# Loads of the first expert tile's weights tied, chunk by chunk, to successive attention units

## The chip, the cores and the metric

The kernel runs on one core of one Trainium2 chip. The metric is device time in microseconds (us) of that core; a time that is quoted alone is the median of several runs. The profile is one further execution. The matmul engine is called PE, its weight loads PEld, the vector engine DVE, the scalar engine ACT, GpSimd POOL, and the queue from which most DMAs are issued SP.

## The reference: what is computed

Three stages follow one another on 1536 tokens (2 batches of 768, 8 heads of 64). The first is attention in which a query sees only the keys of its own cluster, the second a mixture of 8 experts with one expert per token, the third a two-layer network with a leaky nonlinearity.

```python
mask = q_assign[:, :, :, None] == k_assign[:, :, None, :]
scores = scale * np.matmul(q, k.transpose(0, 1, 3, 2))
attn = softmax(np.where(mask, scores, -1e9)) @ v        # shortened
...
e_idx = np.argmax(x @ w_gate + modality_bias[modality_id], axis=1)
h = np.maximum(x[mask] @ w1[e], 0.0)                    # for every expert e
out[mask] = gate_w[mask, None] * (h @ w2[e])
...
h = x @ w_in
return (np.maximum(h, 0) + alpha * np.minimum(h, 0)) @ w_out
```

## The kernel before

**Attention.** The work is cut into 8 groups (2 batches of 4 head pairs), each of 12 units; a unit is one block of 128 queries against one head's 768 keys. A unit's scores are matmuls on PE (line 944, four of them), then DVE takes the row maximum (951), ACT the exponential (963), the result is split into a high and a low half-precision part (`p`), SP issues one transposing DMA (`pt<-p`, line 980), and PE multiplies the transposed tile with the values (line 988, 12 matmuls). The group before its use is prepared beside this (lines 719 to 911, with copies `s2k<-mt` and `s2q<-mt` by DMA, line 389). After a group its output goes to DRAM (`x_d<-xg`, line 1026). After four groups the batch is routed: logits (1045) and a long chain of small DVE operations that ends in tables of tokens and experts.

**Experts.** Tokens are handled in tiles of 128 with one expert each: 5 tiles of the first batch, 8 main tiles after both. A tile is called a slot. The weights of its expert, 4 MB, go in 8 loads of 512 KB (line 1310) into one buffer `wst` of 8 chunks, chunks 0 to 3 for the first layer (matmuls of line 1379), 4 to 7 for the second (line 1409). The loads of slot 0 always run. Those of every later slot are conditional: they move data only if the expert differs from the slot's before, but they are issued, in order, and wait until the chunk's last reader is done. Slots 0, 1 and 2 multiply straight from `wst`, in single-precision matmuls of two records each, and are meant to lie beside the second batch's attention. From slot 3 on the weights are split into `whl` tiles by ACT and DVE (lines 364 and 392) first. Two weight tiles of the third stage are also prepared in this phase (`wst2`, `tw`, `wf`, lines 1453 to 1470).

**What sets the order.** The program is not written in execution order. Every step is an operation with a priority and a set of predecessors; a planner (`Sched.run`) simulates the engines with costs that are written in the kernel, always picks the operation that can start first, and emits all instructions in the order so found. A predecessor given through `deps` moves the operation in that order; it adds no semaphore. The instruction order on each engine is then fixed, and every engine, SP's queue included, takes its instructions in order. The knobs sit in a table `N`; `units` is a list that collects the score operation of every unit, so `units[57]` is the scores of unit 57. Units 0 to 47 are the first batch.

Of the kernel before, what the change touches and what calls it, by code (L numbers as in the profile page):

```python
# [299 lines left out]
def kernel(  # L300
# [17 lines left out]
    B, H, SEQ, D = q.shape  # L318
# [27 lines left out]
    VW = 2 * D + 2  # L346
    CEXP = 15.0 * math.log(2.0)
    BIG = float(2.0 ** 60)
    N = dict(s1q=2, s1k=2, s2q=2, s2k=2, p=3, p16=5, pt=4, v16=2, wf_early=2, xs=2, whl=3, whl2=3, whi='A', wlo='D', lead=1, tw=1, wdma=1.25, pss=2, ps1=4, sq=1, bd=1.5, bp=0, ulead=4, pa=2, pb=0, nat=3, hi='*', lo='DP', vraw=1, mvp=1, mvb=0, epi=1, rM=2, lob=0.5, mve='PA', wd=0.3, wa=0.03, wp=0.03, wpl=0.03, cs=1, back=2, nld=8, dsame=0.127, lump='cs', mp=90, mps=8, mpn=0, trp=0.5, evp=3, xTs2=0, xtp=9, fl=6, rsh=1, rp0=0, go=-4, so=0, pre=0, fws=5, gs=4, gsl=1, xsl=0)
    W_EARLY = N["wf_early"]  # L350

    S = Sched()
    S.back = N["back"]
    S.DSAME = N["dsame"]
    S.win = {"DVE": N["wd"], "ACT": N["wa"], "PE": N["wp"], "POOL": N["wpl"]}
    S.bias = {"DVE": N["bd"], "POOL": N["bp"]}
    MV = {"SP": 0.65, "POOL": 1.05} if N["mvp"] else {"SP": 0.65}
    mv_bias = {"POOL": N["mvb"]}
# [38 lines left out]
    def open_pool(name, side="left", space=None, deps=()):  # L397
        def fn(_):
            kw = dict(name=name, bufs=1, side=side)
            if space is not None:  # L400
                kw["space"] = space
            else:
                kw["reuse_waits"] = "tile"
            p = tc.alloc_tile_pool(**kw)
            pools[name] = p
            for r, shape, dt, n in specs.get(name, ()):
                if isinstance(r, Ring):
                    r.tiles += [p.tile(shape, dt, name=f"{r.name}{len(r.tiles) + i}") for i in range(r.n if n is None else n)]
                else:
                    r.t = p.tile(shape, dt, name=r.name)  # L410

        o = S.op({"MEM": 0.0}, fn, deps=deps, prio=-1e9)
        for r, _, _, n in specs.get(name, ()):
            if n is not None:
                o.adds += tuple((r, r.n + i) for i in range(n))
                continue
            r.opened = o
            if isinstance(r, Buf):
                r.state = {None: ([o], [])}
        return o  # L420

    def close_pool(name):
        deps = set()
        for r, _, _, _ in specs.get(name, ()):
            deps.update(r.ops)
            deps.add(r.opened)
        return S.op({"MEM": 0.0}, lambda _: pools.pop(name).release(), deps=deps, prio=-1e9)
# [10 lines left out]
    def tens(pool, name, shape, dt):  # L438
        b = Buf()
        b.name = name  # L440
        specs.setdefault(pool, []).append((b, shape, dt, None))
        return b
# [32 lines left out]
    fl = tens("const", "fl", [P, B, SLOTS[1]], I32)  # L475
# [202 lines left out]
    units = []  # L678
# [237 lines left out]
    pslot = 8.0  # L916
# [370 lines left out]
        r0 = (b * SLOTS[0] + j) * P  # L1287
        return ys_d[r0:r0 + P, :]

    def slot(b, j, p0, always=False, split=False):  # L1290

        S.prio = p0
        S.stream = "moe"
# [1 line left out]
        nl = 8 // N["nld"]  # L1295
        for c0 in range(0, 8, nl):
            def load(e, c0=c0):
                if not reg:
                    reg.append(nc.sync.value_load(ei.t[0:1, b, j:j + 1], min_val=0, max_val=E - 1))
                    if not always:  # L1300
                        reg.append(nc.sync.value_load(fl.t[0:1, b, j:j + 1], min_val=0, max_val=1))
                kw = {} if always else dict(cond=reg[1] > 0)
                dst = wst.t[:, c0:c0 + nl, :]
                if c0 < 4:
                    src = w1[bass.ds(reg[0], 1), c0 * P:(c0 + nl) * P, :].rearrange("a (k p) f -> p (a k) f", p=P)
                else:
                    src = w2[bass.ds(reg[0], 1), (c0 - 4) * 2 * P:(c0 - 4 + nl) * 2 * P, :].rearrange(
                        "a (k p) f -> p (a k) f", p=P)
                    dst = dst.rearrange("p c (k f) -> p (c k) f", k=2)
                nc.sync.dma_start(dst, src, **kw)  # L1310

            S.op({"SP": 0.6 if c0 == 0 else 0.06}, load, r=[(ei, b), (fl, b)], w=[(wst, c0 + x) for x in range(nl)],
                 dma=((2.95 if always else N["wdma"]) * nl / 2, "load"), prio=p0 - 5)
        xs = S.new(r_xs)
        S.op({"POOL": 1.05}, lambda e: nc.gpsimd.indirect_dma_start(
            out=xs.t, out_offset=None, in_=x_d[0:(b + 1) * SEQ, :],
# [12 lines left out]
        whl = []  # L1329
# [76 lines left out]
        for f in range(KF):  # L1406
            def mm2(e, f=f):
                for i, (a, w_) in enumerate(parts):
# [5 lines left out]
                 prio=p0 + (pslot + 0.1 if split and f >= N["fl"] else 0.3))  # L1414
# [138 lines left out]
    NU = len(groups) * UG  # L1553
# [27 lines left out]
    for b in range(B):  # L1581
        for j in range(MAIN[b]):
            m = b * MAIN[0] + j
            if m == N["nat"]:
                o = close_pool("prep")
                o2 = open_pool("moe2", side="right", deps=[o])
                o = close_pool("core")
                o.deps.add(o2)
                open_pool("moe3", side="right", deps=[o, o2])
                open_pool("ffn0", deps=[o])  # L1590
                open_pool("ffnw", deps=[o])

                open_pool("ps2", space=PSUM, deps=[close_pool("pss")])
            slot(b, j, N["mp"] + N["mps"] * m if b == 0 and m < N["mpn"] else NU + 4 + pslot * m, always=m == 0, split=m >= N["nat"])
            rel.append(last[0])

    S.op({"POOL": 0.6}, lambda e: nc.gpsimd.memset(zt.t, 0.0), w=[zt], prio=NU + 4 + pslot * N["nat"])
# [1 line left out]
    for i, (b, j) in enumerate(spare):  # L1599
# [4 lines left out]
         deps=[last[0]])  # L1604
# [20 lines left out]
    with tc.If(nb[B] > 0):  # L1625
        for b in range(B):
            for j in range(MAIN[b], SLOTS[b]):
                with tc.If(nb[b] > j):
                    slot(b, j, 0.0, always=True)
                    now()  # L1630
        for t in range(C):
            gather(t, x2[0], posu, t)
        now()
# [59 lines left out]
```

## Time and profile before

| What | Value |
|---|---|
| median of 3 runs | 768.56 us (765.15 to 773.28) |
| profiled execution | 769.91 us, span 768.1 us |
| PE busy | 670.0 us (87%) |
| DVE / ACT / POOL busy | 553.9 / 416.3 / 354.3 us |
| moved by DMA | 105.21 MB, mean 137 GB/s |

The span is what lies between the first and last instruction; the remaining 1.8 us of the profiled execution lie around it. The program has four stretches: attention of the first batch (to about 200 us), attention of the second with slots 0 to 2 in it (to about 349), slots 3 to 12 (to about 488), and the third stage, in which PE is busy throughout, to the end. An engine that is busy for a part of a stretch is not what bounds it unless something waits for it; so the rows further down are of waits and of stretches.

### The profile page before, as it was taken

What the parts mean: (1) busy time and instruction counts of PE and PEld (TensorE: products, weight loads), DVE (VectorE), ACT (ScalarE), POOL (GpSimd) and SP (SyncE); (2) the same over time, 40 slices, a digit from 0 to 9 for tenths busy, and PEclk for the clock granted to TensorE, in tenths of its full rate; (3) what the DMA queues carried; (4) which work ended last, traced back from release to release, by engine and by line L of the source; (5) the groups of instructions that cost most, each with busy time, mean ns of one, the idle gap of its engine ahead of it and who ended that gap; (6) DMA issues with size and microseconds to landing.
All of it is one profiled execution on the core that took longest, in us unless ns stands there. A gap on an engine that the chain in (4) does not pass through costs nothing. (4 is left out here: it accounts for less than half of the span.)

```text
span 768.1 us, 11996 instructions
## 1 busy us (share of the span) xinstructions
PE 670.0 (87%) x4135; PEld 561.5 (73%) x4135; DVE 553.9 (72%) x902; ACT 416.3 (54%) x677; POOL 354.3 (46%) x333
## 2 busy tenths in 40 slices
PE   4667777777578898899979989799999999999997
PEld 3656667667466766656857878699999988999996
DVE  7798897989868997469999989488888733332231
ACT  6678777687567968547868988122223232111112
POOL 4258676858357866401244320255645643222221
PEclk9899988988679999999999999999999999999999
DMA  7479999979799979991463651134334030000002
GB/s 178 121 134 209 207 198 174 214 128 226 176 193 231 213 147 185 208 359 45 166 227 101 216 210 70 58 115 141 129 110 134 32 110 28 1 0 1 1 1 82
DMA packets 189284, 105.21 MB, mean 137 GB/s; under 512 B 156480, under 2 KB 169920, under 8 KB 189216
## 3 DMA queue, kind: packets, MB, share of 16 engines
q1 hardware_dynamic: 186848, 96.88, 53.5%
q0 software_dynamic: 2368, 7.49, 3.7%
q8 instruction: 35, 0.57, 0.3%
q14 instruction: 33, 0.27, 0.1%
HBM read 87.37 MB, written 12.85 MB: 130 GB/s over the span
## 5 line engine op out<-in xcount | busy, mean ns | idle before, releaser
L1523 PE MATMUL ps<-wf,ghl 128*128 128x512 f32 x576 | 138.2, 392 | 3.1 <-POOL ghl L392 3.1
L1523 PEld LDWEIGHTS ps<-wf,ghl 128*128 128x128 f32 x576 | 107.0, 188 | 25.5 <-POOL ghl L392 4.6
L392 POOL TENSOR_TENSOR ghl<-g,ghl 128x384 fp32r<-128x384 f32 x62 | 70.6, 1145 | 108.1 <-ACT ghl L364 108.0
L364 ACT ACTIVATE ghl<-g 128x384 fp32r<-128x384 f32 x64 | 33.7, 526 | 140.9 <-DVE g L1506 140.6
L1503 DVE TENSOR_SCALAR m<-ps,alp 128x384 f32<-128x384 f32 x64 | 39.3, 614 | 96.8 <-PE ps L1495 94.3
L951 DVE TENSOR_REDUCE nm<-pss 128x1 f32<-128x768 f32 x96 | 90.7, 950 | 19.8 <-PE pss L944 10.6
L963 ACT ACTIVATE p<-pss,nm 128x768 f32<-128x768 f32 x96 | 86.2, 902 | 34.2 <-DVE nm L951 20.1
L392 DVE TENSOR_TENSOR whl<-wst,whl 128x1024 fp32r<-128x1024 f32 x80 | 100.7, 1299 | 3.0 <-ACT whl L364 2.7
L988 PEld LDWEIGHTS <-pt 128*128 128x128 f16 x1152 | 62.3, 102 | 54.4 <-DMA pt<-p 43.5
L988 PE MATMUL ps<-v,pt 128*128 128x129 f16 (+1 forms) x1152 | 70.8, 214 | 32.1 <-DMA pt<-p 29.1
L392 POOL TENSOR_TENSOR p<-p,p 128x768 f16<-128x768 f32 x48 | 83.1, 1737 | 23.3 <-ACT p L364 13.0
L364 ACT ACTIVATE whl<-wst 128x1024 fp32r<-128x1024 f32 x80 | 83.6, 1059 | 13.1 <-PE ps L1409 5.5
L944 PE MATMUL pss<-s1k,s1q 128*128 128x384 f32 x192 | 63.8, 416 | 13.3 <-ACT p L963 13.0
L1495 PE MATMUL ps<-x2a,wf 128*128 128x384 f32 x384 | 69.9, 338 | 1.8 <-ACTq L1625 1.8
L1495 PEld LDWEIGHTS ps<-x2a,wf 128*128 128x128 f32 x384 | 67.7, 188 | 3.3 <-ACTq L1625 2.2
L1495 PE MATMUL ps<-x2b,wf 128*128 128x384 f32 x384 | 69.9, 338 | 0.0
L1495 PEld LDWEIGHTS ps<-x2b,wf 128*128 128x128 f32 x384 | 67.6, 188 | 1.1
L1379 PE MATMUL ps<-whl,xTs 128*128 128x512 f32 x240 | 63.9, 400 | 4.0 <-DVE whl L392 3.8
L1409 PE MATMUL ps<-whl,hTs 128*128 128x512 f32 x240 | 63.0, 399 | 2.4 <-DVE hTs L392 2.3
L373 POOL TENSOR_SCALAR p<-p 128x768 f16<-128x768 f32 x44 | 41.1, 938 | 39.7 <-ACT p L963 27.8
L976 DVE SCALAR_TENSOR_TENSOR p<-p,p 128x768 f16<-128x768 f32 x48 | 58.7, 1234 | 0.1
L944 PE MATMUL pss<-s2k,s2q 128*128 128x384 f32 x192 | 53.7, 363 | 4.3 <-DMA s2q<-mt 4.3
(238 smaller groups left out, 1140.1 us busy)
## 6 DMA issues: line engine op xcount, KB each, us to landing
wst<-in_moe_w_dram SPq DMA_DIRECT2D x104, 512.0 KB
wst<-in_moe_w_in_dram SPq DMA_DIRECT2D x8, 1024.0 KB
wst<-in_moe_w_out_dram SPq DMA_DIRECT2D x8, 1024.0 KB
ys_d<-ys SPq DMA_DIRECT2D x13, 256.0 KB
raw<-in_k_dram SPq DMA_DIRECT2D x8, 384.0 KB
raw<-in_q_dram SPq DMA_DIRECT2D x8, 384.0 KB
vraw<-in_v_dram SPq DMA_DIRECT2D x8, 384.0 KB
x_d<-xg SPq DMA_DIRECT2D x8, 384.0 KB
```

The lines of the kernel that those rows point to most:

```text
L364: nc.scalar.activation(out=out, in_=in_, func=AF.Copy)
L373: nc.gpsimd.tensor_scalar(out=out, in0=in_, scalar1=1.0 if scale is None else scale, scalar2=0.0, op0=ALU.mult, op1=ALU.add)
L392: ENG[e].tensor_tensor(out=out, in0=a, in1=b, op=ALU.subtract)
L944: nc.tensor.matmul(s.t[:, jj, 0:HS], hd["12"[i], "q"].t[:, h, j, qs], hd["12"[i], "k"].t[:, h, jj], start=(i == 0), stop=(i == 1))
L951: S.op({"DVE": c_dve(SEQ)}, lambda e: nc.vector.tensor_reduce(out=nm.t, in_=s.t[:, :, 0:HS], axis=AX.XY, op=ALU.max, negate=True), r=[s], ...
L963: S.op({"ACT": c_act(SEQ) + 0.04}, lambda e: nc.scalar.activation(out=p.t, in_=s.t[:, :, 0:HS], func=AF.Exp, bias=nm.t), r=[s, nm], w=[p])
L976: S.op({"DVE": c_dve(SEQ)}, lambda e: nc.vector.scalar_tensor_tensor(out=p16.t[:, 1, :], in0=pf(), scalar=PSC, in1=p16.t[:, 0, :], op0=ALU ...
L988: nc.tensor.matmul(o[:, cc, w], p16t(pt)[:, i, :], v16.t[:, tile_of(i % C), h, w], start=(i == 0), stop=(i == 2 * C - 1))
L1379: nc.tensor.matmul(hps[jj].t, lhs(xT, a, ci), rhs(ch, w_, cols), start=(ci == 0 and i == 0), stop=(ci == 3 and i == len(parts) - 1))
L1409: nc.tensor.matmul(yp.t, lhs(hT, a, f), rhs(4 + f // 2, w_, slice((f % 2) * 512, (f % 2 + 1) * 512)), start=(f == 0 and i == 0), stop=(f = ...
L1495: nc.tensor.matmul(hp.t[:, 0:HS], wi[:, a, kk, fs], x2b.t[:, bb, kk, sl], start=(n == 0), stop=(n == 3 * KD - 1))
L1523: nc.tensor.matmul(view(), gh.t[:, a, tt * P:(tt + 1) * P], wo[:, bb, f % 2, :], start=(f == 0 and a == 0 and bb == 0), stop=(f == NF - 1 ...
```

## The change

The table `N` gets a knob `pace=57`. The function `slot` takes it as an argument, which only slot 0 is given, and makes each of its 8 load operations a successor of one unit's scores: the load of chunk 0 follows unit 57, that of chunk 1 unit 58, and so on to chunk 7 and unit 64. Nothing else is edited, but the planner makes a new order of everything from there on.

```diff
-... lob=0.5, mve='PA', ...
+... lob=0.5, pace=57, mve='PA', ...
...
-    def slot(b, j, p0, always=False, split=False):
+    def slot(b, j, p0, always=False, split=False, pace=None):
...
             S.op({"SP": 0.6 if c0 == 0 else 0.06}, load, r=[(ei, b), (fl, b)], w=[(wst, c0 + x) for x in range(nl)],
-                 dma=((2.95 if always else N["wdma"]) * nl / 2, "load"), prio=p0 - 5)
+                 dma=((2.95 if always else N["wdma"]) * nl / 2, "load"), prio=p0 - 5,
+                 deps=[] if pace is None else [units[pace + c0]])
...
-            slot(b, j, ..., always=m == 0, split=m >= N["nat"])
+            slot(b, j, ..., always=m == 0, split=m >= N["nat"], pace=N["pace"] if m == 0 else None)
```

**SP's queue where slot 0's loads begin.** `w1` is the first layer's weights; the transposes `pt` feed the attention. Before:

```order
L980 DMA_TRANSPOSE pt1_160<-p163_157 128x12x128
L1299 TENSOR_LOAD ei_101
L1299 ISA x2
L1310 ISA
L1310 DMA wst_131<-in_moe_w1_dram 128x1024
L1310 ISA
L1310 DMA wst_131<-in_moe_w1_dram 128x1024
L1310 ISA
L1310 DMA wst_131<-in_moe_w1_dram 128x1024
L1310 ISA
L1310 DMA wst_131<-in_moe_w1_dram 128x1024
L389 DMA s2k1_150<-mt0_200 32x2x768
```

After:

```order
L1310 DMA wst_131<-in_moe_w1_dram 128x1024
L389 DMA s2k1_150<-mt0_200 32x2x768
L389 DMA s2q1_148<-mt0_200 16x768
L980 DMA_TRANSPOSE pt2_161<-p164_158 128x12x128
L980 DMA_TRANSPOSE pt3_162<-p160_154 128x12x128
L1310 ISA
L1310 DMA wst_131<-in_moe_w1_dram 128x1024
L980 DMA_TRANSPOSE pt0_159<-p161_155 128x12x128
```

Two loads in place of four stand ahead of the copies and transposes, the third follows two transposes. Counted by the transposes issued ahead of them, slot 0's 8 loads stood at 54 (four), 60, 62 (two) and 68; they now stand at 54 (two), 56, 62 (two), 68 and 78 (two).

**SP's queue where slot 1's conditional loads stand.** Before, six of them in a row after transpose 78:

```order
L980 DMA_TRANSPOSE pt1_160<-p162_156 128x12x128
L1299 TENSOR_LOAD ei_101
L1299 ISA x2
L1301 TENSOR_LOAD fl_102
L1301 ISA x2
L1310 ISA
L1310 DMA wst_131<-in_moe_w1_dram 128x1024
```

After, at that place:

```order
L980 DMA_TRANSPOSE pt1_160<-p162_156 128x12x128
L1310 ISA
L1310 DMA wst_131<-in_moe_w2_dram 128x2x512
L1310 ISA
L1310 DMA wst_131<-in_moe_w2_dram 128x2x512
L980 DMA_TRANSPOSE pt2_161<-p163_157 128x12x128
```

The last two loads of slot 0 took their place. Of slot 1's conditional loads three now stand after transpose 86 and five after the last, the 96th; before it was six and two.

**PE's queue behind the last value product of the attention (line 988).** `xT_134` and `xT_135` are the inputs of slots 2 and 1, `hT_137` a hidden layer, `x3` counts equal rows. Before:

```order
L988 MATMUL ps_3476<-v_164,pt_162 128x65
L1409 MATMUL ps_67<-wst,hT_137 128x512 x3
L1035 MATMUL ps_3478<-ident,xg_180 128x128 x3
L1409 MATMUL ps_67<-wst,hT_137 128x512
L1045 MATMUL ps_66<-wg,xt_181 128x8 x6
L1379 MATMUL ps_65<-wst,xT_134 128x512 x2
```

After (line numbers are one higher from line 1313 on):

```order
L988 MATMUL ps_3447<-v_164,pt_162 128x65
L1380 MATMUL ps_66<-wst,xT_135 128x512
L1380 MATMUL ps_67<-wst,xT_135 128x512
L1403 MATMUL ps_3449<-ident,hb_136 128x128 x4
L1035 MATMUL ps_3450<-ident,xg_180 128x128 x3
L1410 MATMUL ps_64<-wst,hT_137 128x512
L1045 MATMUL ps_65<-wg,xt_181 128x8 x6
L1403 MATMUL ps_3448<-ident,hb_136 128x128 x4
L1324 MATMUL ps_3447<-ident,xs_132 128x128 x4
L1410 MATMUL ps_64<-wst,hT_137 128x512
```

Before, four products of slot 1's second layer were left at that point; now two of its first layer, all eight of its second, the two transposes between and slot 2's input transposes are. Six more such products follow the last row shown, and then slot 2 as before.

## Rows read from the trace of the kernel before

**Rows 1.** The page's head and its busy row.

```profile
span 768.1 us, 11996 instructions
PE 670.0 (87%) x4135; PEld 561.5 (73%) x4135; DVE 553.9 (72%) x902; ACT 416.3 (54%) x677; POOL 354.3 (46%) x333
```

**Rows 2.** Busy time by stretch, with granted clock (1.00 full), DMA share, GB/s.

```profile
core 0: us, PE busy (x) PEld busy (x) DVE busy (x) ACT busy (x) POOL busy (x), PEclk, DMA share, GB/s
205.00:220.00 15.00, 7.83 (x31) 5.48 (x30) 9.05 (x17) 8.24 (x13) 6.83 (x7) 0.50 1.15 187
225.00:325.00 100.00, 89.82 (x778) 67.70 (x775) 80.86 (x138) 76.57 (x140) 68.60 (x63) 1.00 1.05 201
345.00:455.00 110.00, 101.06 (x485) 78.44 (x484) 105.00 (x125) 87.45 (x114) 35.49 (x24) 1.00 0.46 163
640.00:700.00 60.00, 60.00 (x308) 55.15 (x307) 18.82 (x32) 8.41 (x16) 15.62 (x16) 1.00 0.00 1
```

**Rows 3.** SP's queue by time: start, us it was occupied, DMA, count.

```profile
199.76 2.41 SPq L1310 DMA_DIRECT2D wst<-in_moe_w_dram  x4
203.73 0.70 SPq L389 DMA_DIRECT2D s2k<-mt  x1
205.17 15.20 SPq L980 DMA_TRANSPOSE pt<-p  x4
...
271.53 4.01 SPq L980 DMA_TRANSPOSE pt<-p  x2
277.94 2.27 SPq L1310 DMA_DIRECT2D wst<-in_moe_w_dram  x6
280.32 0.68 SPq L389 DMA_DIRECT2D s2k<-mt  x1
281.11 0.56 SPq L389 DMA_DIRECT2D s2q<-mt  x1
281.75 22.40 SPq L980 DMA_TRANSPOSE pt<-p  x10
```

**Rows 4.** Stretches of 5 us around the two sets of loads, columns as in rows 2.

```profile
200.00:205.00 5.00, 3.35 (x21) 2.62 (x22) 4.90 (x19) 2.50 (x7) 1.53 (x2) 0.66 0.77 244
205.00:210.00 5.00, 3.25 (x9) 1.83 (x7) 3.97 (x11) 4.47 (x7) 4.67 (x5) 0.50 1.09 258
275.00:280.00 5.00, 4.96 (x50) 4.32 (x50) 4.87 (x10) 4.59 (x10) 1.93 (x3) 1.00 0.52 98
280.00:285.00 5.00, 5.00 (x23) 3.22 (x21) 4.70 (x12) 3.63 (x7) 4.64 (x5) 1.00 0.70 132
```

**Rows 5.** PE by time, 212 to 231 us; in brackets idle time and its releaser.

```profile
212.51 0.98 PE L944 MATMUL pss<-s2k,s2q 128*128 128x384 f32 x2 [3.77 <-DMA s2q<-mt]
...
218.49 1.16 PE L988 MATMUL ps<-v,pt 128*128 128x129 f16 x12 [2.91 <-DMA pt<-p]
...
230.84 1.88 PE L1379 MATMUL ps<-wst,xT 128*128 128x512 f32 x4
```

**Rows 6.** PE by time, from attention's last product to slot 3's first.

```profile
326.19 0.69 PE L988 MATMUL ps<-v,pt 128*128 128x129 f16 x12 [2.29 <-DMA pt<-p]
326.72 2.82 PE L1409 MATMUL ps<-wst,hT 128*128 128x512 f32 x6
...
336.58 0.65 PE L1402 MATMUL ps<-ident,hb 128*128 128x128 f32 x4
...
341.05 0.60 PE L1323 MATMUL ps<-ident,xs 128*128 128x128 f32 x4
...
348.75 0.48 PE L1379 MATMUL ps<-whl,xTs 128*128 128x512 f32 x1
```

**Rows 7.** DVE by time: route's first step, slot 3's first split, later steps.

```profile
332.07 0.21 DVE L1049 TENSOR_TENSOR lgt<-ps,lgt 128x48 f32<-128x48 f32 x1 [4.65 <-PE ps L1045]
...
348.57 1.22 DVE L392 TENSOR_TENSOR whl<-wst,whl 128x1024 fp32r<-128x1024 f32 x1
...
389.19 0.68 DVE L1465 TENSOR_SCALAR tw<-wst 128x1024 int32<-128x1024 int32 x1
389.90 1.23 DVE L1468 SCALAR_TENSOR_TENSOR tw<-wst,tw 128x1024 int32<-128x1024 int32 x1
391.16 1.22 DVE L1470 SCALAR_TENSOR_TENSOR tw<-wst,tw 128x1024 int32<-128x1024 int32 x1
392.30 6.52 DVE L392 TENSOR_TENSOR whl<-wst,whl 128x1024 fp32r<-128x1024 f32 x3
```

**Rows 8.** Waits by total, 345 to 505 us: us, times, longest.

```profile
PEld ps L1379 <- DVE whl L392: 6.4, 7, 1.7
PEld ps L1409 <- DVE hTs L392: 5.2, 7, 1.4
...
PE ps L1379 <- DVE whl L392: 3.8, 6, 1.2
```

More of the change, by code (lines that the diff above doesn't have):

```diff
@@ L348 @@
     BIG = float(2.0 ** 60)
-    N = dict(s1q=2, s1k=2, s2q=2, s2k=2, p=3, p16=5, pt=4, v16=2, wf_early=2, xs=2, whl=3, whl2=3, whi='A', wlo='D', lead=1, tw=1, wdma=1.25, pss=2, ps1=4, sq=1, bd=1.5, bp=0, ulead=4, pa=2, pb=0, nat=3, hi='*', lo='DP', vraw=1, mvp=1, mvb=0, epi=1, rM=2, lob=0.5, mve='PA', wd=0.3, wa=0.03, wp=0.03, wpl=0.03, cs=1, back=2, nld=8, dsame=0.127, lump='cs', mp=90, mps=8, mpn=0, trp=0.5, evp=3, xTs2=0, xtp=9, fl=6, rsh=1, rp0=0, go=-4, so=0, pre=0, fws=5, gs=4, gsl=1, xsl=0)
+    N = dict(s1q=2, s1k=2, s2q=2, s2k=2, p=3, p16=5, pt=4, v16=2, wf_early=2, xs=2, whl=3, whl2=3, whi='A', wlo='D', lead=1, tw=1, wdma=1.25, pss=2, ps1=4, sq=1, bd=1.5, bp=0, ulead=4, pa=2, pb=0, nat=3, hi='*', lo='DP', vraw=1, mvp=1, mvb=0, epi=1, rM=2, lob=0.5, pace=57, mve='PA', wd=0.3, wa=0.03, wp=0.03, wpl=0.03, cs=1, back=2, nld=8, dsame=0.127, lump='cs', mp=90, mps=8, mpn=0, trp=0.5, evp=3, xTs2=0, xtp=9, fl=6, rsh=1, rp0=0, go=-4, so=0, pre=0, fws=5, gs=4, gsl=1, xsl=0)
     W_EARLY = N["wf_early"]
@@ L1593 @@
                 open_pool("ps2", space=PSUM, deps=[close_pool("pss")])
-            slot(b, j, N["mp"] + N["mps"] * m if b == 0 and m < N["mpn"] else NU + 4 + pslot * m, always=m == 0, split=m >= N["nat"])
+            slot(b, j, N["mp"] + N["mps"] * m if b == 0 and m < N["mpn"] else NU + 4 + pslot * m, always=m == 0, split=m >= N["nat"], pace=N["pace"] if m == 0 else None)
             rel.append(last[0])
```

## The prediction

> **What bounds the kernel now.** I read the page first: PE is busy for 87% of the span and no other engine for more than 72% [rows 1]. That is a mean over stretches with different limits, so the second view is the busy time by stretch. In the last stretch PE has no idle time at all [rows 2]; nothing that the change reorders can shorten it, and it only starts earlier or later. The question is therefore when slot 12 ends, and the change can reach that through the attention of the second batch and through slots 3 to 12. In the second batch's attention PE is busy for 89.8 of 100 us, and the DMA share is above 1 [rows 2]: nearly everything is in use, so a hole is worth looking for, and a plain shift of work is not. From 345 to 455 us DVE is busy for 105.0 of 110 us and PE for 101.1 [rows 2], and PE's named waits there are for DVE's splits [rows 8]: here DVE leads and PE follows.
>
> The third view is SP's queue by time, with the 5 us stretches beside it. At 199.76 us SP issues four weight loads at once; the copies and four transposes behind them are issued from 203.73 on, and those four occupy SP for 15.20 us [rows 3]. [...] A second hole lies at 275.5 us: SP has finished two transposes, and the six conditional loads of slot 1 are issued only at 277.94 us and occupy it for 2.27 us [rows 3]. They move nothing: six loads would be 3 MB, and 98 and 132 GB/s over 5 us each [rows 4] are 1.15 MB for everything together. So slot 1 has the expert of slot 0, and what these loads cost is SP's place in the queue.
>
> **The change, part by part.** No instruction of slot 0 is added or taken away, and no semaphore. What changes is the order, first on SP.
>
> *The burst at 200 us.* Two loads instead of four stand ahead of the copies and transposes. Two loads are 1.05 MB; the queue moved 244 and 258 GB/s while they ran [rows 4], about 251, so 1.05 MB are 4.2 us. The work behind is late by that, and PE has 3.77 and 2.91 us of waits there to give back [rows 5]. Bounds: nothing, if the two loads, which still pass before transpose 78, push back as much later as they release here, since the DMA share is above 1 throughout [rows 2]; and at most 6.2 us, since four transposes took 15.20 us where ten later took 22.40 us, 2.24 each [rows 3], so 15.20 less 9.0. I take 4.2, because the stall is a chain in which every engine stood, and the loads' later places lie between transposes whose units are already ahead. [...]
>
> *The hole at 277 us.* At this place stand now two real loads, the last of slot 0, and no conditional ones. The wait from 275.54 (271.53 + 4.01) to 277.94 us, 2.4 us, was for slot 0's readers and falls away, and so do 2.27 us of issue [rows 3]; three conditional loads come back before the last unit group's output, half of 2.27 or 1.1 us. That releases up to 3.5 us. Against it stand two loads at 2.1 us each, 4.2 us, if nothing hides them. The cover is the hole itself, where the DMA share was 0.52 and 0.70 [rows 4]; if it is gone they cost the difference. Bounds: 3.5 us won to 0.7 us lost. I take 1.5 won, near the middle.
>
> So attention's last value product, at 326.19 us now [rows 6], should come 5.7 us earlier.
>
> *Work pushed behind the attention.* This is the price. Because slot 1's conditional loads now come late, its products do too. Behind the last value product PE has two products of the first layer and eight of the second to do, where four were left: six more. Six records, three products, took 2.82 us [rows 6], so a product is 0.94 us and six are 5.6 us. Two groups of transposes of 0.65 us and the input transposes of slot 2, 0.60 us [rows 6], are added to them: 1.9 us. Together 7.5 us between attention's end and slot 3's first product, which before lay 348.75 - 326.88 = 21.9 us behind it [rows 6]. PE had almost no idle time in those 21.9 us, so this is all on its path; the cover that it had before, PE's waits for transposed tiles such as the 2.29 us ahead of the last one [rows 6], is given up. Slot 3 starts on PE at 348.75 - 5.7 + 7.5, about 350.6 us.
>
> *What DVE does with that time.* DVE's chain of routing steps runs from 332.07 to the first split of slot 3 at 348.57 us [rows 7], and it depends on attention's end, not on slot 1. It should end 5.7 us earlier, and then PE arrives 7.5 us after it. DVE can use them: the first splits of slot 3, as soon as slot 2's first layer has read the chunks, and the three steps on a weight tile of the third stage, 0.68 + 1.23 + 1.22 = 3.1 us [rows 7], one of which the new order puts into the routing chain itself. Four splits of 1.22 us [rows 7] and these are 8.0 us of work. PE was idle for 110 - 101.06 = 8.9 us from 345 to 455 us [rows 2], mostly behind DVE [rows 8]. Bounds: nothing, if the splits wait for chunks that slot 2 still reads; 7.5 us, the whole lead. I take 5, because the steps that move are plain DVE work without another releaser, while PE's idle time holds some waits that are not DVE's.
>
> *The rest at nothing.* A few copies change engines (moves between ACT, POOL and SP, five small differences in the third stage from POOL to DVE); they lie beside PE's continuous work [rows 2]. [...]
>
> Sum: - 4.2 - 1.5 + 7.5 - 5 = - 3.2 us. Against the profiled execution's 769.91 us that is 766.7. Its time stands 1.35 us above the median of the three runs, so I predict a median of **765 us**.
>
> **The rivals.**
>
> *The holes close altogether.* Every stalled engine stood in the burst, and if nothing replaces the stall, the bounds apply: - 6.2 - 3.5 - 7.5 + 7.5 = - 9.7 us, a median of 759. For it speaks that the bytes that are moved later fall into the hole at 277 us; against it that DMA and PE are both near full from 225 to 325 us [rows 2], so late loads should be felt.
>
> *Held back too long, slower.* The loads are moved from a place where they were 31 us early (issued at 199.76, first used at 230.84 us [rows 3, 5]) to places close to their use: the last two are issued directly behind transpose 78, and the new order lets the second layer of slot 0 begin behind that unit's value product. PE takes its instructions in order, so a late chunk holds the scores behind it. The price: two loads of 2.1 us less two products of 0.94 us that run first, 2.3 us. With no gain at the burst, none on DVE and the 7.5 us behind the attention, that is + 9.8 us, a median of 778. It decides as soon as the gains before slot 3 and on DVE together fall short of 7.5 us, and passes 1% only if they are about nothing. For it: the bytes are the same and the queue is full. Against it: the measured 15.20 us for four transposes. [...]
>
> *It cancels.* The DMA work is only shifted (nothing at the burst and at 277 us), and DVE gives back just what PE is late by: 768 to 769. That it leaves the order alone can be excluded; the order did change.
>
> **How the numbers follow.** A measurement of this kernel can tell about 1% from no change, 7.7 us; so faster is below 760.9 and slower above 776.2 us. Forecast 0.43, closed holes 0.24, cancelling 0.15, held back 0.18. Faster takes most of the second and a little of the forecast's own spread, whose terms at their bounds reach 10 us: 0.26. Slower takes nearly all of the last: 0.17. Within 1%: 0.57. The range is 755 to 777 us: it holds the forecast, the cancelling and the middle of the fast rival, and leaves out the upper part of the slow one and the lowest part of the fast, together not more than 0.2.
>
> **What would show it.** The four transposes behind the first loads should occupy SP for about 11 us instead of 15.20, and PE's two waits there shrink. No stop of SP for conditional loads should stand near 275 us. Attention's last value product should start near 320.5 us, slot 3's first product near 350, about 29 us behind it, with DVE's first split ahead of it by several us, and PE should be idle for about 4 us in the 110 us that follow. I am wrong if the last value product is not earlier than 325 us, if PE waits for a weight load in slot 0's second layer, or if DVE starts its splits no earlier than PE comes free.

## The result: 1 to 1.5% slower

The changed kernel took 778.63 us (median of 4 runs, 777.65 to 786.63) against 769.09 us for the kernel before; the ratio is 1.0150, 95% interval 1.0103 to 1.0197. Repeated later on another occasion (run e5) it was 1.0100, 1.0065 to 1.0134. Medians are of all runs; the ratios leave out runs that were disturbed and longer, so the two do not divide exactly. The forecast was 765 us. The number of the rival "held back too long", 778, was met in part by luck: the late chunk that it priced did not come, and the wait at a branch that it did not name did.

The profiled execution took 778.28 us. Its page begins:

```profile
span 776.6 us, 11974 instructions
PE 680.2 (88%) x4135; PEld 572.6 (74%) x4135; DVE 553.0 (71%) x907; ACT 417.5 (54%) x674; POOL 350.9 (45%) x328
```

PE is busy for 10 us more than in [rows 1] with the same number of PE instructions. That says little about the change: 4.0 of the 10 us lie in the stretch ahead of the first difference in order, and the kernel before was itself busy for 675.4 us in a later trace (e15). The busy time of the stretches of [rows 2], columns as there:

```profile
205.00:220.00 15.00, 10.99 (x68) 9.38 (x69) 13.13 (x22) 10.43 (x16) 11.13 (x9) 0.65 0.98 207
225.00:325.00 100.00, 84.96 (x737) 64.53 (x736) 77.28 (x136) 72.25 (x128) 63.91 (x60) 0.96 1.04 204
345.00:455.00 110.00, 104.00 (x488) 80.63 (x488) 102.13 (x125) 89.24 (x115) 35.00 (x23) 0.98 0.49 170
640.00:700.00 60.00, 59.65 (x303) 54.10 (x302) 18.82 (x32) 9.38 (x18) 15.73 (x16) 1.00 0.04 14
```

At 205 to 220 us PE works for 10.99 us where it worked for 7.83: the burst is relieved. But from 225 to 325 us it works less than before (84.96 against 89.82 us), and the attention ends only 1.0 us earlier. SP's queue, as in [rows 3] (start, us it was occupied, DMA, count):

```profile
201.17 1.33 SPq L1310 DMA_DIRECT2D wst<-in_moe_w_dram  x2
...
206.58 4.39 SPq L980 DMA_TRANSPOSE pt<-p  x2
211.19 1.10 SPq L1310 DMA_DIRECT2D wst<-in_moe_w_dram  x1
...
271.78 4.11 SPq L980 DMA_TRANSPOSE pt<-p  x2
276.09 1.54 SPq L1310 DMA_DIRECT2D wst<-in_moe_w_dram  x2
...
300.97 0.99 SPq L1310 DMA_DIRECT2D wst<-in_moe_w_dram  x3
```

A transpose behind the first loads now costs 2.2 us instead of 3.8, and there is no stop near 275 us. PE by time, the places of [rows 5, 6]:

```profile
213.98 1.14 PE L988 MATMUL ps<-v,pt 128*128 128x129 f16 x12 [2.66 <-DVE vsc L906]
...
237.23 1.96 PE L1380 MATMUL ps<-wst,xT 128*128 128x512 f32 x4
...
323.69 2.23 PE L988 MATMUL ps<-v,pt 128*128 128x129 f16 x24
325.73 3.10 PE L1380 MATMUL ps<-wst,xT 128*128 128x512 f32 x4
...
355.35 2.88 PE L1380 MATMUL ps<-whl,xTs 128*128 128x512 f32 x10
```

The value product that waited for a transpose until 218.49 us comes at 213.98. Yet the attention's last ones end at 325.9 us, 1.0 us before those of [rows 6], and slot 3 starts 29.4 us behind that end instead of 21.9. DVE, as in [rows 7], and the waits of [rows 8]:

```profile
332.48 0.21 DVE L1049 TENSOR_TENSOR lgt<-ps,lgt 128x48 f32<-128x48 f32 x1 [6.02 <-PE ps L1045]
...
349.89 1.22 DVE L392 TENSOR_TENSOR whl<-wst,whl 128x1024 fp32r<-128x1024 f32 x1
...
351.71 4.62 DVE L392 TENSOR_TENSOR whl<-wst,whl 128x1024 fp32r<-128x1024 f32 x4
```

```profile
PEld ps L1410 <- DVE hTs L392: 6.4, 7, 2.5
...
PE ps L1410 <- DVE hTs L392: 3.8, 3, 2.0
...
PEld ps L1380 <- DVE whl L392: 0.4, 1, 0.4
```

DVE's first split is 5.5 us ahead of slot 3's first product. The waits for weight splits fall from 6.4 to 0.4 us; those for the split of the hidden layer (`hTs`) do not, they grow from 5.2 to 6.4. Last, the passage from slot 12 to the third stage, which the prediction did not look at: the conditional block for spare tiles is jumped over there. `ACTq` is ACT's sequencer, which takes that branch. PE in the kernel before, then in the changed one:

```profile
489.50 4.46 PE L1495 MATMUL ps<-x2a,wf 128*128 128x384 f32 x24 [1.77 <-ACTq L1625]
```

```profile
495.91 7.28 PE L1496 MATMUL ps<-x2a,wf 128*128 128x384 f32 x24 [4.61 <-ACTq L1626]
```

PE waits 2.8 us longer for ACT's queue, and the 24 products behind the wait take 2.8 us longer. Ten us from the first product on, before and after (columns as in [rows 2]):

```profile
489.50:499.50 10.00, 7.55 (x35) 6.05 (x35) 6.58 (x7) 1.05 (x2) 5.66 (x5) 1.00 0.25 74
```

```profile
495.90:505.90 10.00, 9.92 (x35) 8.92 (x35) 3.78 (x6) 1.05 (x2) 4.40 (x5) 0.69 0.21 56
```

The granted clock is 0.69 over these ten us, behind a pause of PE of 4.61 us: it was 0.50 from 496 to 502 us and 1.00 from 503 us on. Behind 1.77 us it stayed at 1.00. This need not come from the longer pause: when the kernel before ran again (e15), PE paused for 1.81 us at the branch, the clock fell to 0.50 some 7 us later, around a second pause of 2.32 us, and the third stage took 281.2 us from its first product on, against 280.7 in the changed kernel and 278.6 in the first trace. Twenty us from that product on, in e15 and in the changed kernel:

```profile
486.00:506.00 20.00, 17.66 (x76) 15.47 (x77) 12.26 (x15) 2.63 (x4) 8.74 (x7) 0.83 0.28 90
```

```profile
495.90:515.90 20.00, 18.61 (x82) 17.29 (x83) 10.42 (x14) 3.17 (x5) 11.46 (x9) 0.84 0.27 81
```

**Where the 8.5 us of span come from.** Executions differ by some us before anything that the change touches: transpose 54 starts at 192.25 us before and 193.63 after. So I count from its start, in all traces with the order of the kernel before (it, e4, e15) and with the changed order (it, e3, e5, e6, e9):

| us, mean (from, to) | order before | changed order | difference | forecast |
|---|---|---|---|---|
| transpose 54 to the attention's end | 133.7 (132.2, 134.6) | 132.7 (131.8, 133.9) | -1.0 | -5.7 |
| to slot 3's first product (the tail) | 22.0 (21.9, 22.4) | 29.5 (28.8, 30.3) | +7.4 | +7.5 |
| to slot 12's end | 139.0 (138.9, 139.1) | 136.2 (135.4, 137.7) | -2.8 | -5 |
| sum | 294.8 | 298.4 | +3.6 | -3.2 |
| PE's wait at the branch | 1.8 (two traces) | 4.6, 4.9 (the kernel itself) | +3.0 | 0 |

In the profiled pair: 1.4 before transpose 54, 2.2 to slot 12's end, 2.8 at the branch, 2.1 in the third stage, together 8.5 us. The first and the last of these are not shown to be the change's: up to transpose 54 the order is the same on every engine, and the third stage, from its first product on, took 278.4 to 280.7 us (mean 279.3) in the four traces in which ACT stalls at the branch (see e5, e6, e9) and 277.7 to 281.2 us (mean 278.9) in the twelve that have the branch and no stall. The clock fell within its first 20 us in all four, and in five of the twelve. So the traces show 3.6 us to slot 12's end and 3.0 at the branch, 6.6 us. The medians differ by 8.4 us (e5) and 9.5 us, and the intervals begin at 5.0 and 7.9 us; the cause of the rest is open.

### The profile page after: what moved, and what is told of

Its sections match the earlier page's. It is cut to its first block, busy times and chain, and to the rows that moved or that the text cites. A ratio compares the mean times of both kernels' runs of the same rounds, so it can differ in the third digit from the quotient of the medians.

```text
span 776.6 us, 11974 instructions
## 1 busy us (share of the span) xinstructions
PE 680.2 (88%) x4135; PEld 572.6 (74%) x4135; DVE 553.0 (71%) x907; ACT 417.5 (54%) x674; POOL 350.9 (45%) x328
## 5 line engine op out<-in xcount | busy, mean ns | idle before, releaser
L392 POOL TENSOR_TENSOR ghl<-g,ghl 128x384 fp32r<-128x384 f32 x57 | 66.1, 1163 | 119.6 <-ACT ghl L364 119.5
L988 PEld LDWEIGHTS <-pt 128*128 128x128 f16 x1152 | 65.9, 106 | 49.6 <-DMA pt<-p 36.8
L988 PE MATMUL ps<-v,pt 128*128 128x129 f16 (+1 forms) x1152 | 74.6, 220 | 28.6 <-DMA pt<-p 22.5
L1496 PE MATMUL ps<-x2a,wf 128*128 128x384 f32 x384 | 72.7, 347 | 4.6 <-ACTq L1626 4.6
L1496 PEld LDWEIGHTS ps<-x2a,wf 128*128 128x128 f32 x384 | 70.5, 195 | 6.2 <-ACTq L1626 5.0
L373 POOL TENSOR_SCALAR p<-p 128x768 f16<-128x768 f32 x45 | 43.0, 957 | 35.8 <-ACT p L963 23.3
L392 POOL TENSOR_TENSOR wf<-tw,wf 128x1024 fp32r<-128x1024 f32 x16 | 40.3, 2517 | 39.1 <-ACT wf L364 39.0
```

The lines of the kernel that those rows point to most:

```text
L392: ENG[e].tensor_tensor(out=out, in0=a, in1=b, op=ALU.subtract)
L988: nc.tensor.matmul(o[:, cc, w], p16t(pt)[:, i, :], v16.t[:, tile_of(i % C), h, w], start=(i == 0), stop=(i == 2 * C - 1))
L1496: nc.tensor.matmul(hp.t[:, 0:HS], wi[:, a, kk, fs], x2b.t[:, bb, kk, sl], start=(n == 0), stop=(n == 3 * KD - 1))
```

## Experiments

Theories at the start: **A**, the burst's relief is lost within the attention, and the push behind it is paid; **B**, a large part comes at the branch. Rivals: the relief carries and something else costs; DVE pays everything back; the branch only shows what is late. The ratios are to the kernel before on the same occasion. The edits are shown shortened: `ld` are slot 0's loads, `tr` the transposes, `norm` DVE's last step on the norms.

| Run | us | ratio, 95% interval |
|---|---|---|
| e1 two loads spread | 768.99 | 1.0001 (0.9971 to 1.0031) |
| e2 slot 1 pushed | 774.88 | 1.0078 (1.0041 to 1.0116) |
| e3 changed, no branch | 770.03 | 1.0021 (0.9991 to 1.0051) |
| e4 before, no branch | 766.44 | 0.9977 (0.9951 to 1.0004) |
| e5 changed again | 776.81 | 1.0100 (1.0065 to 1.0134) |
| e6 changed, 16 ACT steps | 775.04 | 1.0091 (1.0056 to 1.0127) |
| e7 pushed, no branch | 772.42 | 1.0050 (1.0018 to 1.0083) |
| e8 spread, no branch | 767.17 | 0.9969 (0.9938 to 0.9999) |
| e9 changed, 4 ACT steps | 775.09 | 1.0054 (1.0009 to 1.0098) |
| e10 before, slot 1 free | 780.14 | 1.0120 (1.0055 to 1.0185) |
| e11 changed, slot 1 free | 779.48 | 1.0115 (1.0046 to 1.0184) |
| e12 pace=65 | 778.37 | 1.0118 (1.0083 to 1.0153) |
| e13 before, tiny loads | 771.47 | 1.0028 (0.9991 to 1.0064) |
| e14 changed, tiny loads | 778.10 | 1.0134 (1.0073 to 1.0195) |
| e15 before again | 769.07 | one run |
| e16 spread, push by 2 | 770.44 | 1.0012 (0.9977 to 1.0047) |
| e17 changed, 4 steps, POOL held | 772.74 | 1.0017 (0.9987 to 1.0047) |
| e18 spread, POOL held | 769.51 | 0.9987 (0.9952 to 1.0022) |

### The parts alone: e1, e2

```diff
     order = S.run()
+    # e1, on the kernel before: slot 0's loads 2 and 3 behind transposes 56 and 60
+    for i, at in ((3, 60), (2, 56)):
+        order.remove(ld[i]); order.insert(order.index(tr[at - 1]) + 1, ld[i])
```

> The kernel before, with two loads of slot 0 moved in SP's queue alone: the third behind transpose 56, the fourth behind transpose 60; PE's and DVE's order untouched, slot 1 untouched. Theory A (the relief at 200 us is real but lost before the attention ends, since other chains pace that stretch): PE's waits at 212 and 218 us shrink by about 4 us together, attention's last value product comes 0 to 1 us earlier, slot 3's first product near 348, median 767 to 770. Rival (the prediction's step: the relief carries through): last value product near 322, slot 3 near 344.5, median near 765. Rival (spread loads hurt where they now stand): slot 0's first product late, slot 3 after 350, median 772 or more.

```diff
-            ... prio=p0 - 5)
+            ... prio=p0 - 5, deps=[units[{0: 88, 3: 94}[c0]]] if m == 1 and c0 in (0, 3) else [])   # e2
```

> The kernel before, slot 0's loads where they were, but slot 1's conditional loads tied to late units, so that the same two products of its first layer and all eight of its second lie behind the attention as in the changed kernel. Theory A (the push is paid in full at slot 3 and about 3 us of it come back in slots 3 to 12): slot 3 starts 29 us behind the last value product, near 355, the last product of slot 12 about 4 us later than in the kernel before, median 773 if the branch is passed as before, up to 779 if it also costs what it did in the changed kernel. Rival (DVE's lead pays it all back): slot 12 ends as in the kernel before, median 768 to 770.

e1 changes nothing that can be measured, as theory A said. Its stretch to the attention's end is 132.0 us, 1.7 below the mean of its order, and 133.9 in e8: a us or so in the mean, not 4. e2 costs 6 us. Its tail is 28.9 us and slots 3 to 12 take 134.1 (139.0 before), so the push is paid in full and 4.9 us come back: theory A in kind. Those two make some 2 us, not 6, so one trace does not account for the median. (That execution took 768.72 us, 6.2 less than the median of its kernel.)

### Without the branch: e3, e4, e7, e8

The same lines are left out of the changed kernel (e3), the kernel before (e4) and the kernels of e2 and e1 (e7, e8):

```diff
-    nb = [nc.values_load(nsl2.t[0:1, b:b + 1], min_val=0, max_val=SLOTS[1]) for b in range(B + 1)]
-    with tc.If(nb[B] > 0):
...
-        now()
     S.prio = 0
```

> The changed kernel without the conditional block for spare tiles between slot 12 and the third stage (nothing in it runs with this data). Theory B (some 5.6 of the 8.5 us come at the branch: 2.8 us more idle time of PE and 2.8 us at half clock behind it): the start of the third stage follows slot 12 within 2 us at full clock, median 768 to 771, and it is only 3 to 4 us above the same cut of the kernel before. Rival (the branch only shows what is late anyway): median 774 or more, still 8 to 9 us above the same cut of the kernel before.

> The kernel before without the same conditional block. Theory B: the branch there cost 1.8 us of idle time and no half clock, so the median falls by 1 to 3 us, to 766 to 768. Rival (the block costs nothing or its removal reorders the start of the third stage for the worse): 769 or more.

> The kernel with slot 1 held back and slot 0's loads as before, without the conditional block for spare tiles, which does nothing with this data; to be read against the kernel before without that block (766.4). Theory A (the push costs about 7 us at slot 3 and 3 to 5 of them come back by slot 12): 2 to 4 us above, 768.5 to 770.5. Rival (the push explains the whole change): 775 or more. Rival (DVE's lead pays all of it): 766 to 767.

> The kernel before with only the third and fourth load of slot 0 moved behind transposes 56 and 60, without the conditional block; to be read against the kernel before without that block (766.4). Theory A (the relief of the burst is lost before the end): 765.5 to 767. Rival (the relief of 2 to 4 us from the first load to the attention's end that one trace shows carries through, and was hidden by the spread of the runs): 762.5 to 764.5.

e3 is 3.6 us above e4, where the kernels themselves are 8 to 9.5 us apart: theory B, within its forecast. In the traces of the two, slot 12 ends 297.3 and 293.7 us after the start of transpose 54, the same 3.6 us. e7 stays 6.0 us above e4, above theory A's 2 to 4. e8 is no faster than e4 (767.17 and 766.44), so the relief of two loads does not carry.

### ACT's place in its program: e5, e6, e9

In the changed kernel's trace ACT's first instruction behind its branch comes 2.96 us after the branch ended, in the kernel before 0.41 us. ACT had executed 831 instructions by then, against 847. Theory **C**: the place decides, not what the queues hold.

> The changed kernel once more, beside the others on one chip. Theory C (ACT's stall behind the branch belongs to where ACT's program lies and is there in every execution): 3 us again between ACT's branch and its next instruction, PE idle for more than 4 us ahead of the third stage, median 777 to 780. Rival (chance of that one execution): ACT goes on within 0.5 us of its branch as in the kernel before, median 770 to 774.

```diff
     order = S.run()
+    o = [o for o in order if o.on == "ACT"][-1]
+    o.fn = lambda e, fn=o.fn: ([copy("ACT", tiny.t, tiny.t) for _ in range(16)], fn(e))   # e9: range(4)
```

> The changed kernel with 16 tiny ACT instructions (copies of one 128x1 tile onto itself, idle time of ACT covers them) ahead of ACT's last copy of slot 12. ACT has executed 831 instructions before the branch in the changed kernel, 847 in the kernel before: with the 16 the branch stands at 847 again. Theory C: ACT goes on within 0.5 us of the branch, PE waits about 1.8 us for the third stage, no half clock in its first 10 us, median 770 to 773. Rival (the stall comes from the load order, or from what the queues hold at that time): 3 us stall and 778 again.

> The changed kernel with 4 tiny ACT instructions ahead of ACT's last copy of slot 12 in place of 16: ACT executes 835 instructions before the branch, one more than in the kernel with slot 1 held back (834, no stall), four more than in the changed kernel (831, stall of 3 us). Theory C (ACT's place in its program decides): ACT goes on within 0.5 us, PE waits about 2 us, third stage from slot 12's end to the end of the span 280 to 281 us instead of 284.5 to 285.3, median 772 to 775. Rival (the 16 copies helped by the time they took): stall of 3 us and 777 again.

PE's first product of the third stage in e5, e6 and e9:

```profile
499.22 1.03 PE L1496 MATMUL ps<-x2a,wf 128*128 128x384 f32 x3 [4.91 <-ACTq L1626]
```

```profile
492.27 4.40 PE L1496 MATMUL ps<-x2a,wf 128*128 128x384 f32 x24 [2.13 <-PEq L1628]
```

```profile
496.20 4.43 PE L1496 MATMUL ps<-x2a,wf 128*128 128x384 f32 x24 [1.81 <-ACTq L1628]
```

Theory C holds for the stall. ACT stalls for 3.28 us in e5, for 0.41 us in e6 and e9, and the 24 products are back at 4.4 us. Over all runs: at 831 and 832 executed instructions (the changed kernel, e5, e14, e11) ACT goes on after 2.4 to 3.3 us; at 834 to 848 (e2, e9, e17, e10, e12, e16, the kernel before, e1, e6, e13, e15, e18) after 0.41 or 0.42. The medians fall only by 1.8 us from e5 and lie above both forecasts (770 to 773 and 772 to 775), and the intervals of e5, e6 and e9 overlap, so the runs do not show what the stall is worth. The traces give a size: from slot 12's end to the end of the span it is 282.4 to 285.3 us (mean 283.8) in the four with the stall, and 279.7 to 283.0 (mean 280.9) in the twelve with the branch and without the stall, 2.9 us less.

### Fewer and more products behind the attention: e10, e11, e12, e16

```diff
+            if (b, j) == (0, 1):    # e10 and e11: no loads for slot 1
+                continue
             S.op({"SP": 0.6 if c0 == 0 else 0.06}, load, ...
```

> The kernel before without slot 1's 8 conditional loads (they move nothing with this data, slot 1 has slot 0's expert): the products of slots 1 and 2 move up, 14 products lie behind the attention instead of 20, and the stop of SP at 275 us is gone. Theory D (the push and what DVE pays back are two sides of one balance: PE ahead of DVE gains nothing): slot 3 starts 5 to 6 us nearer to the attention's end, slots 3 to 12 take 4 to 6 us longer, median 766 to 769. Rival (every product behind the attention costs its 0.94 us): 762 to 764.

> The changed kernel without slot 1's conditional loads: slot 0's loads spread as in the changed kernel, 16 products behind the attention instead of 26. ACT executes 832 instructions before the branch. Theory A (the push is what the changed kernel lost before slot 12, the spread itself gives about 1 us): slot 12 ends 286 to 287 us after slot 0's first load, as in the kernel before or 1 us earlier, against 290 in the changed kernel; median 766 to 769 if ACT passes the branch, 771 to 773 if it stalls there as at 831. Rival (the late loads themselves cost): slot 12 ends 289 us or more after the first load.

```diff
-pace=57
+pace=65     # e12
```

> The changed kernel with the first load tied to unit 65 instead of 57: 34 products behind the attention instead of 26, the loads later still; ACT executes 843 instructions before the branch, so no stall is expected there. Theory A with D (0.94 us per product pushed, DVE's payback ends where PE's idle time of 8.9 us does): slot 3 starts 13 to 15 us later behind the attention than in the kernel before, 5 to 7 us come back, median 774 to 778. Rival (payback goes on in step): 769 to 771.

e16 is e1 with slot 1's first conditional load tied to unit 84.

> The kernel before with the third and fourth load of slot 0 behind transposes 56 and 60, and slot 1's conditional loads held back a little, so that 22 products lie behind the attention instead of 20; ACT executes 843 instructions before the branch, no stall expected. Theory D (20 products are where PE's work and DVE's routing chain of 22 us balance, each further one costs PE 0.94 us and gets half of it back): 768 to 770, no better than the kernel before. Rival (a little lead for DVE is worth more than it costs): 764 to 766.

My theory D failed at e10 and e11, and usefully. With 14 products behind it, the tail in e10 is still 21.6 us, while the stretch to the attention's end takes 142.3 us instead of 133.7. PE in e10:

```profile
334.64 0.68 PE L988 MATMUL ps<-v,pt 128*128 128x129 f16 x12
...
345.48 5.32 PE L1411 MATMUL ps<-wst,hT 128*128 128x512 f32 x12
353.74 0.35 PE L1086 MATMUL ps<-T,M 128*128 128x19 f16 x2 [2.95 <-DVE M L1084]
...
356.96 0.77 PE L1381 MATMUL ps<-whl,xTs 128*128 128x512 f32 x1
```

PE is out of products at 350.8 us and waits for DVE's routing steps. So the routing chain sets a floor of about 22 us; up to 20 products lie beside it for nothing, and the kernel before had exactly 20. In e12, with 34, the tail is 36.6 us, 14.6 longer; 6.7 us come back (132.3 in slots 3 to 12) and the attention ends 3.9 us sooner. That is the limit that D gave. The trace is 4.0 us slower by this sum, the ratio 9 us; the profiled execution took 772.02 us, 6.4 less than the median of its kernel. e16 (22 products) has a tail of 23.7 us and is no better than the kernel before, as D had it. In e11, with 16 products, the tail is 22.1 us and the attention's stretch 138.4, so slot 12 ends 295 us after the first load, beyond the 289 us from which I had put the rival. Six and ten products more inside the attention came with 8.6 and 5.7 us more of it, in orders that the planner made anew, while six taken out of it give 1.0.

### Bytes or order: e13, e14, e15

```diff
+                if (b, j) == (0, 0):    # e13 on the kernel before, e14 on the changed one
+                    dst, src = dst[..., 0:64], src[..., 0:64]
                 nc.sync.dma_start(dst, src, **kw)
...
     order = S.run()
+    for c, o in enumerate([o for o in order if o.on == "POOL"][40:56:2]):
+        o.fn = lambda e, fn=o.fn, c=c: (nc.gpsimd.memset(wst.t[:, c, :], 0.0), fn(e))
```

Both leave out most of the bytes of slot 0's weights, so slots 0 and 1 multiply other weights than the reference.

> The kernel before, in which slot 0's 8 loads move 64 of the columns of each chunk row only, a sixteenth of w1's bytes and an eighth of w2's (the rest of the chunks is zeroed earlier by POOL, so slot 0 and 1 compute with other weights); every order is unchanged. From the start of transpose 54 to the end of the last value product the kernel before took 134.6 and 132.2 us. Theory A (the bytes of slot 0's loads cost the stretch, wherever they stand): the wait at 212 to 218 us goes, the stretch takes 128 to 130 us, some 4 us less, and the median falls to 764 to 766. Rival (other chains pace the attention): 132 us or more, median 767 to 769.

> The changed kernel with the same tiny loads, order unchanged; its stretch from transpose 54 to the last value product took 131.8 to 133.9 us. Theory A: 127 to 129 us, again some 4 us less, which says that the spread loads cost what the burst cost. Rival (other chains pace it): 131 us or more.

> The kernel before once more, for its trace: from transpose 54's start 132 to 135 us to the attention's end, 22 us to slot 3, 139 us to slot 12's end, PE waits 1.8 us ahead of the third stage, ACT goes on within 0.5 us of the branch.

Us after the start of transpose 54:

| | transpose 66 | transpose 78 | attention's end |
|---|---|---|---|
| order before (3 traces) | 49.8 | 80.2 | 133.7 |
| e13, the same with tiny loads | 45.3 | 76.5 | 130.2 |
| changed order (5 traces) | 47.2 | 80.5 | 132.7 |
| e14, the same with tiny loads | 44.5 | 80.5 | 132.6 |

This splits theory A, as far as one trace of each can. In the order before, the stretch without the bytes of slot 0's loads is 3.5 us below the mean, 2.0 to 4.4 below the single traces, and most of the lead lasts. In the changed order it is at the mean: without the bytes, too, the lead of transpose 66 is gone at transpose 78. So it seems to be the order, not the bytes of the loads, that holds this stretch. (e13's median, forecast at 764 to 766, does not show the 3.5 us; its transpose 54 starts at 195.4 us, 3 to 7 us later than in the other three traces of its order, and POOL zeroes the chunks before that, which may be why.)

### What holds it: e17, e18

DVE, POOL and ACT of the changed kernel where slot 0's products begin:

```profile
232.73 3.25 DVE L754 TENSOR_TENSOR rs<-rn,rs 128x24 f32<-128x24 f32 x1
```

```profile
232.68 3.25 POOL L392 TENSOR_TENSOR p<-p,p 128x768 f16<-128x768 f32 x2
```

```profile
239.27 1.90 ACT L963 ACTIVATE p<-pss,nm 128x768 f32<-128x768 f32 x2 [3.11 <-DVE nm L951]
```

A DVE step on 24 elements per partition takes 3.25 us, from the start to the end of two POOL instructions; ACT then waits 3.11 us for DVE's maxima. In all seven traces of the changed order (with e11, without e17) it is 3.25 or 3.26 us. The kernel before has the collision too, but a smaller one (0.68 us in e4 and e15):

```profile
234.76 1.60 DVE L754 TENSOR_TENSOR rs<-rn,rs 128x24 f32<-128x24 f32 x1
```

```diff
+    # e17 (with e9's 4 ACT steps): POOL's two subtractions behind DVE's norms; e18: one in each of groups 5 and 6
+    order.remove(o); order.insert(order.index(norm) + 1, o)
+    o.fn = lambda e, fn=o.fn: (nc.gpsimd.tensor_scalar(out=nsl2.t[:, 0:1], in0=rn.t[:, 0, 0:1], ...), fn(e))
```

> The changed kernel with the 4 tiny ACT copies (no stall at the branch), and with POOL's two subtractions p<-p,p of group 5 made to wait for DVE's four small steps on the norms (a 128x1 POOL step that reads their result stands ahead of them). To be read against the same kernel without it (775.1, from transpose 54 to the attention's end 131.8 to 133.9). Theory E (POOL holds DVE there, and ACT and PE behind it): the step of 3.25 us takes 0.2 us, transposes 66 to 78 take 31 us or less instead of 32.4 to 35.5, the attention ends 130 to 131.5 us after transpose 54, median 772 to 774. Rival (the place of slot 0's products on PE is what costs): the step is short but transposes 66 to 78 still take 32.5 us or more, and the median stays at 775.

> The kernel before with the third and fourth load of slot 0 behind transposes 56 and 60 (769.0 by itself), and the same hold of one POOL subtraction behind DVE's small steps in groups 5 and 6. Theory E: the two steps of 0.7 and 1.8 us take 0.2 us, the attention ends 130.5 to 132 us after transpose 54, median 766 to 768, 1 to 2 us under the kernel before. Rival (POOL's later start delays its transposes by as much): 768.5 to 770.

The same three steps in e17:

```profile
229.36 0.18 DVE L754 TENSOR_TENSOR rs<-rn,rs 128x24 f32<-128x24 f32 x1
```

```profile
230.34 3.57 POOL L392 TENSOR_TENSOR p<-p,p 128x768 f16<-128x768 f32 x2
```

```profile
233.37 1.90 ACT L963 ACTIVATE p<-pss,nm 128x768 f32<-128x768 f32 x2 [0.93 <-DVE nm L951]
```

The step takes 0.18 us, ACT waits 0.93 us, transposes 66 to 78 take 31.8 us (32.4 to 35.5 with it) and the attention's stretch 131.4 (131.8 to 133.9). Theory E's bound of 31 us for transposes 66 to 78 was missed, so the collision is at most a part of what holds this stretch, and the rest I have not found. The median, 772.74, is in E's range and 2.3 us below e9's, but the two were measured on different occasions, and the intervals of their ratios overlap. In the trace slot 12 ends 298.2 us after the start of transpose 54, where the mean of the changed order is 298.4. So a gain of the whole kernel is not shown.

Nor does the collision separate the two orders by much. One group later (group 6) the same step takes 1.80, 1.76 and 1.33 us in the order before (the kernel itself, e4, e15) and 0.18 to 0.47 in the changed one; over both groups that is 2.0 to 3.4 us before and 3.4 to 3.7 after. In e18 both steps take 0.18 us and the attention's stretch is 131.7, as E forecast, but the median of 769.51 is the rival's (768.5 to 770) and not E's (766 to 768); its ratio is 0.9987 with an interval on both sides of 1. No version here that keeps the branch beats the kernel before.

## Why the prediction was wrong, step by step

- **Burst (-4.2) and hole (-1.5): the step that failed first, by size.** The relief at its place is real, and about 3.5 us is what the bytes of slot 0's loads cost in the order before (e13, one trace). But of 5.7 us only 1.0 arrived at the attention's end. I had argued that "the stall is a chain in which every engine stood", and counted a gain at one place as a gain at the end. Behind that place the new order loses the lead again, and in e14 it did so without the loads' bytes. What holds it there is open: the collision of POOL with DVE (e17) is at most a part.
- **Push (+7.5): right**, +7.4. The reason was half seen: the cover that was given up is DVE's routing chain, 22 us, which 20 products just fill.
- **DVE pays back (-5): too large**, -2.8; e2 and e7, with the same push, got 4.9 and 4.0. DVE's lead, 5.5 us and not 7.5, removed PE's waits for weight splits, and the next wait, for `hTs`, was named nowhere in the sum, although [rows 8] has 5.2 us of it.
- **"The rest at nothing": the step that failed by kind.** I wrote that copies which change engines "lie beside PE's continuous work". But the new order left ACT with 16 instructions fewer ahead of the branch, 3 that work and 13 of its sequencer, and there a stall of 3 us cost PE 3.0 us; it also brought two POOL instructions onto DVE's small step. Neither is a matter of the loads' bytes. That the clock cost another 2 us, as the profiled pair has it, is not shown: PE is busy in the third stage for 273.2 us there and for 273.1 in e15, which has no stall. In the traces the stall hangs on ACT's place in its program, 2.4 to 3.3 us at 831 and 832 instructions and 0.4 at 834 and more; what ACT waits for at that place no run shows.
- **What was to be seen:** no stop near 275 us, 29.4 us of tail and DVE several us ahead (5.5) came as written. Of the four transposes in about 11 us only two stand behind the first loads, in 4.39 us. The last value product near 320.5 us (it was 324.8) and 4 us of PE idle time (6.0 of 110) did not come. No wait for a weight load was seen in slot 0's second layer, so the late chunk of the slow rival did not happen.
- **The sum:** -3.2 forecast to slot 12's end, +3.6 in the traces; the branch made it 6.6. For the 2 to 3 us between this and the medians no cause was found.

## What to carry to other kernels

Where a planner writes the order, a small edit is a new program: look in its order for every join, branch and shared resource downstream, not only for what the edit is about, and price those too. A gain in mid-stream counts only if the next stretch is not paced by something else; leaving the suspect work out (tiny loads) helps to tell. And before pushing work behind a stage, find what already sets the length of the tail: up to that length (here 22 us, 20 products) work was free, beyond it every product was paid (14 in e12 for 14.6 us).

## What the runs showed that I had not expected

- DVE's small step (`rs<-rn,rs`) lasted until POOL's whole instruction beside it was done, and even the next one: 3.25 us in the changed kernel for a step that takes 0.18 in e17. POOL started at 232.68 us and DVE at 232.73, and DVE's step ended only 0.05 us after the second of the two POOL instructions, which followed each other directly. Why DVE is held there no run shows.
- Four tiny ACT instructions ahead of a branch took its stall from 2.96 and 3.28 us to 0.41 (e9).
- Transpose 54, ahead of every edit, starts anywhere from 188.3 to 195.3 us. Traces are best compared from a mark behind such a stretch.
- Left open: why e2 and e7 are 6 us slower when their traces account for 1 to 3, and e12 9 us when its trace accounts for 4; and what holds transposes 66 to 78 in the changed order.
